# Decode attention plus MLP: wq loaded in eight DMAs, and two rows of wo in sixteen DMAs of falling size

## The chip, the cores and the metric

The kernel runs on one core of a Trainium2 chip. The core has a matrix engine (PE), three element-wise engines (DVE, ACT, POOL), a queue engine (SP) that only starts transfers, and sixteen DMA engines that move data between HBM and the on-chip memory SBUF, which has 128 partitions. The metric is device microseconds for one execution. Times before: 1281.98 and 1281.99 us in two runs, median 1281.99 us.

## What is computed

One decode step for 8 sequences (B = 8, one new token each, model width 640): a layer norm, then attention over a cache of 4096 keys with 32 heads of 128, plus a two-layer MLP on the same normalized input, plus the input itself.

```
xn = layernorm(x)                                   # x: 8 x 1 x 640
q  = xn @ wq                                        # wq: 640 x 4096
p  = softmax(q . k_cache / sqrt(128))               # k_cache, v_cache: 8 x 32 x 4096 x 128
A  = (p . v_cache) @ wo                             # wo: 4096 x 640
h  = gelu(layernorm(xn) @ w1 + b1)
out = x + A + h @ w2 + b2
```

All tensors are bf16. The two caches are 268 MB each, so nearly all of the bytes that the kernel moves are K and V, and each is read once.

## The kernel before

The work is cut into 32 groups (`NQ`): 8 heads of one sequence each. A group needs one K tile and one V tile, each 128 partitions x 65,536 bytes, 8 MB. SBUF has three slots of that size: K tiles alternate between two (`KA`, `KB`), V has the third (`VS`). All large transfers are started by SP, in one queue, in an order that is written out by hand: every step is registered with a position (`at(pos, step)`), the steps are sorted by it, and each engine gets its part of the list. A transfer may start when the slot is free: K tile i waits for the compute on K tile i-2 (`load_k`), V tile i for the product with V tile i-1 (`load_v`).

At the start the V slot holds the query weights wq: `load("wq", ...)` is the first transfer in SP's queue, 128 partitions of 40,960 bytes (5 rows of wq each). Behind it comes K tile 0. PE computes all queries from wq in one go (`pe_q`, 160 matmuls); K tile 1 and V tile 0 are issued only when that is done (`qmm`), since their slots hold the inputs. ACT's queue starts the small inputs: x (8 partitions), b2, and the last rows of w2 (`w2b`, 64 partitions).

At the end the output weights wo are loaded into a K slot, when the last K tile has been used. wo is cut by heads: `load_wl(0)` loads the first sixteen heads (2,560 KB), `load_wl(1)` the next eight (1,280 KB), and `load_wn` the last eight in three pieces. In these, a partition holds eight rows of wo (index s, 1,280 bytes each), and `WN_CUT = (0, 5, 7, 8)` cuts them: rows 0 to 4 (800 KB), rows 5 and 6 (320 KB: 128 partitions x 2,560 bytes), row 7 (160 KB). Each piece has its own semaphore, and PE adds it to the sum in `fin_wn(q)` when it has landed: 25, 10 and 5 matmuls. These 40 matmuls are the last real work; then the sum is cast (DVE), transposed (PE), copied (ACT) and stored.

So SP's queue reads: wq, K0, [wait for the queries] K1, V0, then K and V in turn, the MLP weights, V31, and behind the last wait five transfers of wo. A DMA adds 16 to its semaphore in all when it is complete, so that a wait for n DMAs on one semaphore is a wait for 16 n.

## Time and profile before

| | us |
|---|---|
| two timed runs | 1281.98, 1281.99 |
| profiled execution, first to last instruction | 1280.5 |
| DVE busy | 1103.8 |
| PE busy (matmul) | 671.1 |
| ACT busy | 476.6 |
| POOL busy | 106.3 |

The profiled execution is known by its span; the 1.5 us by which the timed runs are longer lie ahead of its first and behind its last instruction. DVE has the largest busy time of the compute engines, but 177 us less than the span. What is read off the profile below is mainly the state of the DMA engines: the share of time that the sixteen are busy, and the rate in GB/s, over the span and in chosen stretches. In a stretch, a packet is counted whole where it starts, so that short stretches give figures that swing, above 1 at places; they are used here over several packets, or where packets are short.

### The profile page before, as it was taken

The numbers are of one execution on the slowest core, as the hardware profiler recorded it, in microseconds if no ns is written. First come the engines' busy times: TensorE is split into PE (matmuls) and PEld (weight loads), VectorE is DVE, ScalarE is ACT, GpSimd is POOL, SyncE is SP. The second block draws the span as 40 slices with busy tenths as digits, with TensorE's granted clock in tenths as the row PEclk, the third lists the DMA queues.
The fourth block names the chain that finished last, engine by engine and source line by source line (L and its number), as shares of the span: only waits on it lengthen the run. The fifth ranks groups of instructions, "written<-read, shape, count | busy, mean of one in ns | idle before, by whom it ended". The sixth has DMA issues, their size and how long they took to land.

```text
span 1280.5 us, 34440 instructions
## 1 busy us (share of the span) xinstructions
PE 671.1 (52%) x13944; PEld 573.4 (45%) x13944; DVE 1103.8 (86%) x680; ACT 476.6 (37%) x904; POOL 106.3 (8%) x113
## 2 busy tenths in 40 slices
PE   1546555446545446545456554456454466464476
PEld 1435444335535345444345444345343355353365
DVE  1899999889888889888899888898888898888895
ACT  0524444233444233443234443234443234442331
POOL 0020010000000000000000000000000000000040
PEclk9755655566665565555565565566655555555655
DMA  9999999999999999999999999999999999999998
GB/s 419 431 426 435 426 436 432 442 426 436 432 440 428 434 432 438 432 432 430 436 438 426 434 434 442 426 434 434 438 430 430 430 440 436 428 432 436 433 437 361
DMA packets 10675, 551.99 MB, mean 431 GB/s; under 512 B 1244, under 2 KB 1445, under 8 KB 1702
## 3 DMA queue, kind: packets, MB, share of 16 engines
q1 hardware_dynamic: 10512, 551.70, 99.7%
q8 instruction: 9, 0.15, 0.0%
q10 hardware_dynamic: 150, 0.11, 0.0%
q14 instruction: 4, 0.03, 0.0%
HBM read 551.80 MB, written 0.01 MB: 431 GB/s over the span
## 4 chain that ended last, share of the span: by engine, by line
DMA 52%; DVE 36%; issue 11%; DVEq 0%; PE 0%; SPq 0%; ACT 0%
DMA S_sb<-in_A_k_cache_dram 51%; DVE S_sb L111 26%; DVE Sd_sb L111 8%; DMA S_sb<-in_A_wo_dram 2%; DVE S_ps L111 1%; DVE ri_sb L111 0%; DVEq L109 0%; PE ACC_ps L111 0%; DVE mx_sb L111 0%; SPq L111 0%; DVE mbT_sb L111 0%; DVE mxT_sb L111 0%; DVE mq_sb L111 0%; DVE mb_sb L111 0%; PE QB_ps L111 0%
## 5 line engine op out<-in xcount | busy, mean ns | idle before, releaser
L111 PE MATMUL TR_ps<-ident_bf,S_sb 128*128 128x128 bf16 (+1 forms) x2570 | 341.2, 273 | 354.1 <-POOL kr_sb L111 333.7
L111 DVE TENSOR_TENSOR S_sb<-S_sb,qbc_sb 128x7552 bf16<-128x7552 bf16 (+1 forms) x96 | 392.5, 4088 | 128.8 <-DMA S_sb<-in_A_k_cache_dram 128.4
L111 PEld LDWEIGHTS TR_ps<-ident_bf,S_sb 128*128 (+2 forms) x2570 | 243.6, 102 | 414.0 <-issue 338.2
L111 DVE TENSOR_REDUCE Sd_sb<-S_sb 128x59 f32<-128x3776 bf16 (+1 forms) x96 | 390.2, 4065 | 6.0
L111 ACT ACTIVATE KT_sb<-TR_ps 128x1024 bf16<-128x1024 bf16 x320 | 327.0, 1024 | 121.1 <-PE TR_ps L111 109.5
L111 PE MATMUL PV_ps<-P_sb,S_sb 128*128 128x8 bf16 x8192 | 224.0, 175 | 137.5 <-DMA S_sb<-in_A_v_cache_dram 134.5
L111 PEld LDWEIGHTS PV_ps<-P_sb,S_sb 128*128 128x128 bf16 x8192 | 221.4, 103 | 140.2 <-DMA S_sb<-in_A_v_cache_dram 137.0
L111 DVE TENSOR_TENSOR S_sb<-S_sb 128x3776 bf16<-128x3776 bf16 (+1 forms) x96 | 205.4, 2140 | 3.3
L111 ACT ACTIVATE P_sb<-Sd_sb,NB_sb 128x256 bf16<-128x256 f32 x256 | 126.3, 494 | 213.7 <-DVE NB_sb L111 213.7
L111 PE MATMUL S_ps<-qrep_sb,KT_sb 128*128 128x8 bf16 x2560 | 121.6, 177 | 51.6 <-ACT KT_sb L111 48.6
L111 ACT ACTIVATE oU_sb<-PV_ps 128x8 f32<-128x8 f32 x31 | 5.5, 178 | 376.8 <-PE PV_ps L111 376.8
L111 PEld LDWEIGHTS S_ps<-qrep_sb,KT_sb 128*128 128x128 bf16 x2560 | 91.3, 102 | 82.2 <-ACT KT_sb L111 41.6
L111 POOL TENSOR_TENSOR oT_sb<-oU_sb,ri_sb 128x8 bf16<-128x8 f32 x31 | 71.8, 2316 | 374.8 <-DVE S_sb L111 303.1
L111 POOL COPY qrep_sb<-qT_sb 128x128 bf16<-128x128 bf16 x32 | 19.2, 600 | 472.6 <-PE S_ps L111 454.0
L111 ACT ACTIVATION_READ_ACCUMULATOR P_sb<-Sd_sb,NB_sb 128x1 f32 x256 | 47.7, 186 | 0.0
L111 DVE TENSOR_TENSOR S_ps<-S_ps,mask_sb 128x320 f32<-128x320 f32 (+1 forms) x65 | 31.6, 486 | 2.6 <-PE S_ps L111 2.6
L111 DVE TENSOR_REDUCE Sd_sb<-S_ps 128x40 f32<-128x320 f32 x64 | 31.5, 492 | 2.2
L111 PE MATMUL QB_ps<-ident_bf,qrep_sb 128*128 128x128 bf16 x32 | 9.2, 286 | 40.7 <-DVE S_sb L111 21.2
L111 ACT ACTIVATE qbc_sb<-QB_ps 128x128 bf16<-128x128 f32 x32 | 8.9, 278 | 56.9 <-PE QB_ps L111 56.9
L111 POOL MEMSET kr_sb<- 128x1 f32 x32 | 3.2, 99 | 295.4 <-DMA S_sb<-in_A_k_cache_dram 295.4
L111 PEld LDWEIGHTS QB_ps<-ident_bf,qrep_sb 128*128 128x128 bf16 x32 | 3.3, 104 | 43.6 <-ACT oU_sb L111 29.3
L111 PE MATMUL CH_ps<-rs_sb,ones_f 128*128 128x8 f32 x64 | 16.7, 335 | 6.5 <-ACT P_sb L111 6.5
(73 smaller groups left out, 148.6 us busy)
## 6 DMA issues: line engine op xcount, KB each, us to landing
S_sb<-in_A_v_cache_dram SPq DMA_DIRECT2D x1, 6144.0 KB, 26.8
S_sb<-in_A_wq_dram SPq DMA_DIRECT2D x1, 5120.0 KB, 15.2
S_sb<-in_A_wo_dram SPq DMA_DIRECT2D x1, 2560.0 KB, 15.8
S_sb<-in_B_w_dram SPq DMA_DIRECT2D x1, 2160.0 KB, 30.3
S_sb<-in_B_w_dram SPq DMA_DIRECT2D x1, 2080.0 KB, 34.8
S_sb<-in_A_v_cache_dram SPq DMA_DIRECT2D x1, 2048.0 KB, 31.3
S_sb<-in_A_wo_dram SPq DMA_DIRECT2D x1, 1280.0 KB, 18.5
S_sb<-in_A_wo_dram SPq DMA_DIRECT2D x1, 800.0 KB, 20.0
```

The costliest lines, as they stand in the source:

```text
L111: inst = getattr(e, name)(*a, **k)
```

## The change

```
     WN_CUT = (0, 5, 7, HS)
+    ROWS_CUT = (15, 14, 13, 12, 11, 10, 9, 8, 8, 7, 6, 5, 4, 3, 2, 1)
...
+        def load_wq():
+            src = A_wq.rearrange("(p c) n -> p c n", c=DC)
+            for r in range(RW):
+                load("wq", ld_wq, wq_sb[r:P:RW], src[r:P:RW])
...
         def load_wn(q):
             lo, hi = WN_CUT[q], WN_CUT[q + 1]
             n = HS * DH
-            tk[("wn", q)] = ld_wn[q].sig(sp.dma_start(
-                woL_sb[:, 1, lo * D:hi * D],
-                A_wo[NL * n:(NL + 1) * n, :].rearrange("(p s) n -> p (s n)", p=P)[:, lo * D:hi * D]))
+            src = A_wo[NL * n:(NL + 1) * n, :].rearrange("(p s) n -> p (s n)", p=P)
+            a = 0
+            for k in ROWS_CUT if lo == WN_CUT[1] else (P,):
+                tk[("wn", q)] = ld_wn[q].sig(sp.dma_start(
+                    woL_sb[a:a + k, 1, lo * D:hi * D], src[a:a + k, lo * D:hi * D]))
+                a += k
...
-        at(-890, load, "wq", ld_wq, wq_sb, A_wq.rearrange("(p c) n -> p c n", c=DC))
+        at(-890, load_wq)
```

`RW` is 8. The one wq transfer of 128 partitions becomes eight transfers of 16 partitions: number r takes the partitions r, r + 8, r + 16 and so on to r + 120. All eight count on the semaphore of wq, and PE waits for the last of them, so for 128 in place of 16. Behind them K tile 0 follows in SP's queue as before.

The 320 KB piece of wo (rows 5 and 6 of the last eight heads) becomes sixteen transfers over consecutive partitions: 15 partitions, then 14, and so on down to 8, a second one of 8, and on to 1; 128 in all. They count on one semaphore, for which PE waits with 256 in place of 16. The 800 KB piece ahead and the 160 KB piece behind stay one DMA each.

Bytes, places in SBUF and all compute instructions are the same; SP's program has 22 more DMA instructions, the other engines' programs are unchanged.

## The prediction

> **What bounds the kernel now.** I read the page first, then SP's timeline, the DMA issues, the stretches, and the end of the chain of waits.

> ```profile
> span 1280.5 us, 34440 instructions
> ...
> DMA  9999999999999999999999999999999999999998
> ...
> q1 hardware_dynamic: 10512, 551.70, 99.7%
> ...
> HBM read 551.80 MB, written 0.01 MB: 431 GB/s over the span
> ```

> The digit line says that the sixteen DMA engines are busy in every slice; SP's queue (q1) alone keeps them busy for 99.7% of the span. The reader is to see that there is no slice with room in it: 551.7 MB at one constant rate are the time. DVE is in the chain of waits too, but what it waits for, and what waits for it, is the next tile. So an edit here is worth what it does to the first byte, to the rate, or to the last byte.

> The columns of the stretches below are the length, the busy time of PE, weight load, DVE, ACT and POOL, the granted clock, the DMA share and GB/s.

> ```profile
> 1.50:14.50 13.00, 1.22 (x21) 0.99 (x21) 5.00 (x22) 1.69 (x3) 0.78 (x8) 1.00 1.01 410
> 8.00:12.00 4.00, 0.56 (x13) 0.42 (x11) 0.18 (x1) 0.00 (x0) 0.00 (x0) 1.00 1.00 432
> 140.00:1240.00 1100.00, 585.85 (x12134) 499.02 (x12134) 970.07 (x566) 426.97 (x810) 86.39 (x86) 0.55 1.00 433
> ```

> From 8 to 12 us wq is under way, in rows of 40,960 bytes; from 140 to 1240 us K and V, in rows of 65,536. Both run at the same 432 to 433 GB/s, 27 GB/s for each of sixteen engines. A rate that doesn't care for the row length is that of a path of fixed width. Up to 14.5 us the mean is 410, so the first stretch of wq costs (1 - 410/432) x 13 = 0.7 us.

> ```profile
> 0.74 0.38 SPq L111 DMA_DIRECT2D S_sb<-in_A_wq_dram  x1
> 1.17 19.60 SPq L111 DMA_DIRECT2D S_sb<-in_A_k_cache_dram  x2
> 20.81 0.43 SPq L111 DMA_DIRECT2D S_sb<-in_A_v_cache_dram  x1
> ```
> ```profile
> 15.98 4.43 PE L111 MATMUL CH_ps<-xT_sb,S_sb 128*128 128x8 bf16 x160 [7.43 <-DMA S_sb<-in_A_wq_dram]
> ```
> ```profile
> S_sb<-in_A_wq_dram SPq DMA_DIRECT2D x1, 5120.0 KB, 15.2
> w2b_sb<-in_B_w_dram ACTq DMA_DIRECT2D x1, 80.0 KB, 13.9
> ...
> S_sb<-in_A_k_cache_dram SPq DMA_DIRECT2D x1, 34.8
> ```

> wq is issued at 0.74 us and lands 15.2 us later, and PE starts on it at 15.98. K0 stands behind it, issued at 1.17 and landed 34.8 us later: the engines go from wq to K0 without a pause. Whatever wq takes longer, everything behind it comes later by the same, since the queue is never empty again.

> **Part 1, wq in eight DMAs.** Removed: one issue of 0.38 us. Added: eight of that kind, 3.0 us, the last ending near 0.74 + 3.0 = 3.8 us. K0's issue moves from 1.17 to about 3.8, and that costs nothing: its bytes are wanted only when wq is through, near 15 us; 11 us of wq cover it. Each later piece has a cover too: a row of 40,960 bytes takes an engine 1.5 us at 27 GB/s, an issue 0.38. K1 and V0 wait for the queries as before, and K0's transfer covers that wait in both cases. The x, b2 and w2b loads go through ACT's queue and are not moved. In POOL's and PE's queues nothing moves, and the wait for 128 in place of 16 stands where the other stood.

> What can cost is the rate. The DMA is cut over the engines by partitions, as x shows, eight partitions, ahead of wq:

> ```profile
> DMA packets 6, 0.01 MB, mean 219 GB/s; under 512 B 0, under 2 KB 6, under 8 KB 6
> ...
> q10 hardware_dynamic: 6, 0.01, 124.8%
> ```

> That is the stretch from 1.700 to 1.735 us: six of its eight 1,280-byte rows start within 35 ns, so on different engines: one row, one engine. A 16-row piece gives each engine one row too. But these are rows 8 partitions apart, and which sixteen of SBUF's rows are written at the same time is new: before, an engine had eight rows of its own out of 128. If the path of fixed width is the engine's own, nothing is lost, and the first stretch may gain: between -0.7 us (its whole loss) and 0. If it is SBUF's side, shared by a set of partitions, then sixteen rows at a regular step need not lie on sixteen paths. With two on one path the rate is 216 GB/s: 5,120 KB (5.24 MB) take 24.3 us in place of 12.1, so +12.1. Bounds: -0.7 and +12.1 us. The rows of before hold no large load but those over 128 partitions, so they don't decide. I take two on one path, because a step of 8 in 128 is as regular as it can be, and each engine's eight pieces follow in the same order, so that two engines that meet go on meeting. From the 12.1 I take off the 0.7 of the slow first stretch, which half the rate hides: **+11.4 us**.

> [...]

> **Part 2, rows 5 and 6 of the last heads.**

> ```profile
> S_sb<-in_A_wo_dram SPq DMA_DIRECT2D x1, 2560.0 KB, 15.8
> S_sb<-in_A_wo_dram SPq DMA_DIRECT2D x1, 1280.0 KB, 18.5
> S_sb<-in_A_wo_dram SPq DMA_DIRECT2D x1, 800.0 KB, 20.0
> S_sb<-in_A_wo_dram SPq DMA_DIRECT2D x1, 320.0 KB, 20.3
> S_sb<-in_A_wo_dram SPq DMA_DIRECT2D x1, 160.0 KB, 20.2
> ```
> ```profile
> L111 SPq DMA_DIRECT2D S_sb<-in_A_wo_dram x5: 328/432/433, 1256.0 to 1257.8; - x5
> ```
> ```profile
> 1256.82 19.96 DMA S_sb<-in_A_wo_dram
> ...
> 1276.82 1.50 PE ACC_ps L111 x40
> ...
> 1278.35 0.21 DVE res_sb L111
> ```
> ```profile
> 1275.28 1.21 PE L111 MATMUL ACC_ps<-oS_sb,S_sb 128*128 128x8 bf16 x40
> 1276.82 1.49 PE L111 MATMUL ACC_ps<-oS_sb,S_sb 128*128 128x8 bf16 x40 [0.34 <-DMA S_sb<-in_A_wo_dram]
> ```

> Five issues of some 0.43 us each run from 1256.0 to 1257.8 (start of the last); sixteen in place of one add 15 x 0.43 = 6.5 us of SP, so the last starts near 1264.3. Its bytes are wanted at 1276 to 1277, when the others are through: about 12 us of V31 and wo cover it. Nothing else stands behind it on SP but the wait for the output. If that cover were gone it would cost up to 6.5 us.

> The chain ends with the 800 KB piece landing at 1276.78, then 40 matmuls. The same 40 took 1.21 us with everything there, and 1.49 here, so 0.28 us are waits for the later pieces: the last, issued at 1257.8, lands 20.2 us on, at 1278.0. A later landing there moves the end one for one; an earlier one gives 0.28 at most, as the 800 KB piece holds the start.

> ```profile
> 1275.50:1276.00 0.50, 0.50 (x25) 0.50 (x22) 0.43 (x2) 0.00 (x0) 0.00 (x0) 0.50 0.99 392
> 1276.00:1276.50 0.50, 0.49 (x19) 0.40 (x15) 0.00 (x0) 0.00 (x0) 0.00 (x0) 0.50 0.80 307
> 1276.50:1277.00 0.50, 0.18 (x6) 0.18 (x7) 0.00 (x0) 0.00 (x0) 0.00 (x0) 0.50 0.66 254
> 1277.00:1277.50 0.50, 0.50 (x25) 0.50 (x22) 0.00 (x0) 0.00 (x0) 0.00 (x0) 0.50 0.47 153
> ```

> The share falls from 0.99 to 0.47 over the last 1.5 us: the engines don't end together. The falling sizes move work: with one row to an engine, counted from the first, the first engine gets a row of all sixteen DMAs and the last none, where each had eight of 2,560 bytes (8 x 2,560 / 27 GB/s = 0.76 us). So the first engine ends 0.76 us later than now, the last 0.76 earlier. Whether the first ones are those that end early the rows don't say. Without meetings, this part gives between -0.28 and +0.76. With meetings, consecutive partitions may share a path: four rows on one, in lock-step, would make sixteen DMAs take 16 x 4 x 2,560 / 27 = 6.1 us, +5.3; the spread of 1.5 us in arrival breaks most of that up. I take half the rate, as for wq, for 320 KB: **+0.8 us**.

> **Sum.** The stretches are of an execution with a span of 1280.5 us; the timed runs are 1.5 us longer, around it, and nothing there changes. 1281.99 + 11.4 + 0.8 = 1294.2 us.

> **The rivals.**
> *No meeting* (not slower): the fixed path is each engine's own. For it: the constant rate fits that just as well. Against it: nothing but the regularity of the step. The time is 1281.99 with -0.7 to 0 for the first stretch and -0.28 to +0.76 for the end: 1281.0 to 1282.8, likeliest 1281.7. It decides as soon as a 16-row piece keeps 27 GB/s per engine.
> *Meeting at the end only*: neighbouring partitions share a path, partitions at a step of 8 or more don't. wq as now, the end +0.8 to +5.3, so 1282.8 to 1287.3, likeliest 1283.5. For it: the pieces of wo are consecutive partitions, those of wq far apart.
> *The pieces are not spread*: a 16-row DMA with this step runs on a quarter of the engines or paths. Then wq takes four times 12.1 us, +36.4, 1318 us. x's six rows in 35 ns speak against fewer engines. It passes 2% (25.6 us) from 0.32 of the rate on.

> **How the numbers follow.** Half rate at wq 0.62; no meeting 0.26; end only 0.07; not spread 0.03; the remaining 0.02 for what I don't see. The first case has a range of its own of 1291.5 to 1296.5 (two engines that meet drift apart and save up to 2; the end up to +3). Leaving out no-meeting would leave out too much, so the range goes from 1281.0 to 1296.5. A change of 2%, 25.6 us, is what is told from no change here; half rate and no meeting both stay under it, on either side of zero. More than 2% faster would need a stretch with idle DMA engines, and there is none: 0.01. More than 2% slower is the piece that isn't spread and unseen things: 0.04. Within: 0.95.

> **What would show it.** Right: the stretch from 8 to 12 us falls from 432 to about 216 GB/s, wq lands near 26.5 us and PE's 160 matmuls start there, K0's landing moves by the same 11 us, the stretch of K and V keeps 433 and its steps keep their length, and SP's sixteen issues end long before the last bytes. In the end the share falls over a longer time, with the 320 KB piece landing 0.8 us later against the 800 KB one. Wrong: 432 from 8 to 12 us and PE starting at 16 us or before; then the rest of the time is in the last 2 us, or a changed step in the middle would say that something other than wq's rate came in.

## The result: 15.5 us slower

The changed kernel takes 1297.51 us (1297.42 and 1297.60 in two runs) against 1281.99 us: +15.52 us, ratio 1.012, interval 1.0103 to 1.0136. The forecast was 1294.2 us with a range up to 1296.5; the direction and the mechanism held, the size did not.

The page of the changed kernel, and its stretches (columns as before: length, busy time of PE, weight load, DVE, ACT and POOL, granted clock, DMA share, GB/s):

```profile
span 1296.0 us, 34462 instructions
...
GB/s 229 440 427 428 435 431 437 431 435 435 431 437 431 435 433 433 435 433 433 435 433 431 435 433 437 433 429 437 433 435 431 433 437 433 431 435 433 429 438 341
...
q1 hardware_dynamic: 10736, 551.70, 99.6%
```
```profile
17.00:26.60 9.60, 0.00 (x0) 0.00 (x0) 0.00 (x0) 0.00 (x0) 0.00 (x0) 1.00 1.00 205
30.00:140.00 110.00, 53.58 (x1059) 45.19 (x1057) 88.70 (x48) 40.81 (x68) 6.76 (x9) 0.69 1.01 434
140.00:1240.00 1100.00, 579.24 (x11942) 492.12 (x11939) 970.27 (x576) 422.67 (x809) 88.54 (x88) 0.57 1.00 433
```

Of the forty slices only the first (229 GB/s, 419 before) has a much lower rate; the last is somewhat lower (341, 361 before). In wq's stretch all sixteen DMA engines are busy all the time, and move 205 GB/s. A busy share of 1.00 therefore says nothing of the rate here, as 432 GB/s had the same share before: in the trace's packet records a row of 40,960 bytes takes an engine 3.13 us in the mean here, and took 1.51 before, and all of it counts as busy. (From 8 to 12 us, the stretch that the forecast names, the view reads 261 GB/s at a share of 1.25, since packets are counted whole where they start; 261 / 1.25 = 209.) K and V run at 433 as they did.

SP's and PE's timelines of the changed kernel, at the start and at the end:

```profile
0.74 5.09 SPq L111 DMA_DIRECT2D S_sb<-in_A_wq_dram  x8
5.87 28.72 SPq L111 DMA_DIRECT2D S_sb<-in_A_k_cache_dram  x2
...
1270.07 7.46 SPq L111 DMA_DIRECT2D S_sb<-in_A_wo_dram  x20
```
```profile
29.80 4.43 PE L111 MATMUL CH_ps<-xT_sb,S_sb 128*128 128x8 bf16 x160 [21.39 <-DMA S_sb<-in_A_wq_dram]
...
1291.94 0.83 PE L111 MATMUL ACC_ps<-oS_sb,S_sb 128*128 128x8 bf16 x25 [1.31 <-DMA S_sb<-in_A_wo_dram]
1293.22 0.56 PE L111 MATMUL ACC_ps<-oS_sb,S_sb 128*128 128x8 bf16 x15 [0.45 <-DMA S_sb<-in_A_wo_dram]
```

PE starts the queries at 29.80 in place of 15.98 us: +13.8. SP's wait for the last K tile ends at 1270.07 in place of 1255.97: +14.1, so nothing was caught up or lost to speak of in 1240 us. The last 40 matmuls end at 1293.78 in place of 1278.31: +15.5. The time went to two places: 13.8 us into wq, some 1.4 us into the end, where the 40 matmuls, one run before, are now broken in two by waits.

### The profile page after: what moved, and what is told of

It is laid out like the page before. It is cut to its first block, busy times and chain, and to the rows that moved or that the text cites. A ratio compares the mean times of both kernels' runs of the same rounds, so it can differ in the third digit from the quotient of the medians.

```text
span 1296.0 us, 34462 instructions
## 1 busy us (share of the span) xinstructions
PE 670.8 (52%) x13944; PEld 572.6 (44%) x13944; DVE 1103.6 (85%) x680; ACT 476.4 (37%) x904; POOL 102.4 (8%) x113
## 2 busy tenths in 40 slices
DMA  9999999999999999999999999999999999999998
## 3 DMA queue, kind: packets, MB, share of 16 engines
q1 hardware_dynamic: 10736, 551.70, 99.6%
HBM read 551.80 MB, written 0.01 MB: 426 GB/s over the span
## 4 chain that ended last, share of the span: by engine, by line
DMA 52%; DVE 35%; issue 11%; SPq 1%; DVEq 0%; PE 0%; ACT 0%
DMA S_sb<-in_A_k_cache_dram 51%; DVE S_sb L111 26%; DVE Sd_sb L111 7%; DVE S_ps L111 1%; DMA S_sb<-in_A_wo_dram 1%; SPq L111 1%; DVE ri_sb L111 0%; DVEq L109 0%; DVE mx_sb L111 0%; DVE mbT_sb L111 0%; DVE mxT_sb L111 0%; DVE mq_sb L111 0%; PE ACC_ps L111 0%; DVE mb_sb L111 0%; PE QB_ps L111 0%
## 5 line engine op out<-in xcount | busy, mean ns | idle before, releaser
L111 PE MATMUL TR_ps<-ident_bf,S_sb 128*128 128x128 bf16 (+1 forms) x2570 | 340.4, 269 | 353.4 <-POOL kr_sb L111 337.8
L111 DVE TENSOR_TENSOR S_sb<-S_sb,qbc_sb 128x7552 bf16<-128x7552 bf16 (+1 forms) x96 | 392.4, 4088 | 129.1 <-DMA S_sb<-in_A_k_cache_dram 128.8
L111 PEld LDWEIGHTS TR_ps<-ident_bf,S_sb 128*128 (+2 forms) x2570 | 242.9, 102 | 414.1 <-issue 337.4
L111 DVE TENSOR_REDUCE Sd_sb<-S_sb 128x59 f32<-128x3776 bf16 (+1 forms) x96 | 390.2, 4065 | 6.0
L111 ACT ACTIVATE KT_sb<-TR_ps 128x1024 bf16<-128x1024 bf16 x320 | 326.9, 1024 | 121.2 <-PE TR_ps L111 109.8
L111 PE MATMUL PV_ps<-P_sb,S_sb 128*128 128x8 bf16 x8192 | 224.8, 175 | 138.8 <-DMA S_sb<-in_A_v_cache_dram 134.7
L111 PEld LDWEIGHTS PV_ps<-P_sb,S_sb 128*128 128x128 bf16 x8192 | 222.4, 103 | 141.5 <-DMA S_sb<-in_A_v_cache_dram 137.4
L111 DVE TENSOR_TENSOR S_sb<-S_sb 128x3776 bf16<-128x3776 bf16 (+1 forms) x96 | 205.4, 2140 | 3.3
L111 ACT ACTIVATE P_sb<-Sd_sb,NB_sb 128x256 bf16<-128x256 f32 x256 | 126.3, 494 | 213.5 <-DVE NB_sb L111 213.5
L111 PE MATMUL S_ps<-qrep_sb,KT_sb 128*128 128x8 bf16 x2560 | 121.9, 178 | 51.3 <-ACT KT_sb L111 48.2
L111 ACT ACTIVATE oU_sb<-PV_ps 128x8 f32<-128x8 f32 x31 | 5.5, 178 | 378.1 <-PE PV_ps L111 378.1
L111 PEld LDWEIGHTS S_ps<-qrep_sb,KT_sb 128*128 128x128 bf16 x2560 | 91.2, 102 | 81.6 <-ACT KT_sb L111 41.5
L111 POOL TENSOR_TENSOR oT_sb<-oU_sb,ri_sb 128x8 bf16<-128x8 f32 x31 | 71.6, 2310 | 379.0 <-ACT oU_sb L111 216.7
L111 POOL COPY qrep_sb<-qT_sb 128x128 bf16<-128x128 bf16 x32 | 15.5, 485 | 487.4 <-PE S_ps L111 454.9
L111 ACT ACTIVATION_READ_ACCUMULATOR P_sb<-Sd_sb,NB_sb 128x1 f32 x256 | 47.8, 187 | 0.0
L111 ACT ACTIVATE qbc_sb<-QB_ps 128x128 bf16<-128x128 f32 x32 | 8.9, 278 | 70.8 <-PE QB_ps L111 70.8
L111 DVE TENSOR_TENSOR S_ps<-S_ps,mask_sb 128x320 f32<-128x320 f32 (+1 forms) x65 | 31.5, 485 | 2.6 <-PE S_ps L111 2.6
L111 DVE TENSOR_REDUCE Sd_sb<-S_ps 128x40 f32<-128x320 f32 x64 | 31.5, 491 | 2.2
L111 PE MATMUL QB_ps<-ident_bf,qrep_sb 128*128 128x128 bf16 x32 | 9.2, 286 | 40.6 <-DVE S_sb L111 22.0
L111 POOL MEMSET kr_sb<- 128x1 f32 x32 | 3.2, 99 | 294.5 <-DMA S_sb<-in_A_k_cache_dram 294.5
L111 DVE CAST qT_sb<-CH_ps 128x256 bf16<-128x256 f32 x1 | 0.4, 424 | 26.1 <-PE CH_ps L111 26.1
L111 PEld LDWEIGHTS QB_ps<-ident_bf,qrep_sb 128*128 128x128 bf16 x32 | 3.3, 104 | 43.4 <-ACT oU_sb L111 28.8
## 6 DMA issues: line engine op xcount, KB each, us to landing
S_sb<-in_A_wo_dram SPq DMA_DIRECT2D x1, 2560.0 KB, 15.8
S_sb<-in_B_w_dram SPq DMA_DIRECT2D x1, 2080.0 KB, 34.8
S_sb<-in_A_wo_dram SPq DMA_DIRECT2D x1, 1280.0 KB, 18.5
```

What stands on the lines that cost most here:

```text
L111: inst = getattr(e, name)(*a, **k)
```

## The experiments

All times are compared with the kernel before as run on the same chip beside them (1282.01 us for the first four, 1281.86 for e5, e6 and e9, 1282.02 for e7 and e8, 1282.06 for the last three). Edits are shown against the kernel before.

**The two parts alone.** e1 has the changed kernel's `load_wq` and the old `load_wn`; e2 the reverse.

> Only wq is cut, into eight DMAs of 16 partitions at a step of 8; wo is loaded as before. If the two parts of the change add up, this has what the changed kernel lost by the start of its 160 query matmuls, 29.80 against 15.98 us, so +13.8: 1295.8 us, and the end as before. If the parts depend on each other (the engines' order at the end being set by the start), the sum of this run and the next differs from +15.5 by more than 0.5 us.

> Only rows 5 and 6 of the last heads are cut, into the sixteen DMAs of 15 to 1 partitions; wq is one DMA. From the changed kernel's end (its last landing to its last matmul, 1.4 us later against the start than before): 1283.4 us. A shared path for neighbouring partitions says +0.8 to +2; if the falling sizes only move work between engines, -0.3 to +0.8.

e1: 1296.21 us, +14.2, ratio 1.0108 (1.0079 to 1.0138). e2: 1284.02 us, +2.0, ratio 1.0015 (1.0004 to 1.0027). The sum, 16.2, is 0.7 above the 15.5 of both together. That passes the 0.5 us that the expectation set as the mark of parts that depend on each other, but e1's interval alone is some 3.8 us wide to either side, so whether they do stays open. wq is the large part.

**The number of DMAs, or the partitions?** e3 cuts wq by columns, e4 into two kinds of 16-row pieces.

```
+            dst, src = (t.rearrange("p c n -> p (c n)") for t in (wq_sb, src))     # e3
+            n = DC * H * DH // RW
+            for r in range(RW):
+                load("wq", ld_wq, dst[:, r * n:(r + 1) * n], src[:, r * n:(r + 1) * n])
...
+            for r in range(4):                                                     # e4
+                load("wq", ld_wq, wq_sb[32 + r:96:4], src[32 + r:96:4])
+            for lo in (0, 96):
+                for r in range(2):
+                    load("wq", ld_wq, wq_sb[lo + r:lo + 32:2], src[lo + r:lo + 32:2])
```

> wq is cut into eight DMAs again, but by columns: each takes all 128 partitions and 5,120 bytes of each. Shared path in SBUF: nothing lost, 432 GB/s from 8 to 12 us, 1281.3 to 1282.7 us. A price for each DMA of a cut transfer (some 1.7 us for each of eight): 1295.8 us.

> wq in eight DMAs of 16 partitions, in two kinds. The first four take partitions 32+r, 36+r and so on to 92+r (step 4 over partitions 32 to 95); the last four take every second partition of 0 to 31 or of 96 to 127. Shared path, with a path for four neighbours that is shared with the partitions 32 further on in the same half of 64: the first four pieces have sixteen paths and run at 432 GB/s, 1.5 us each, the last four have eight paths for sixteen rows, 3.2 us each: half of the loss of e1, +6.9, 1288.9 us. A price for each DMA of 16 rows: 1295.8 us, and the same rate from the first piece on.

e3: 1282.60 us, ratio 1.0004 (0.9992 to 1.0015), no difference to be told. Its stretch from 5 to 15 us, with eight DMAs, and its start of the queries:

```profile
5.00:15.00 10.00, 1.21 (x21) 0.99 (x21) 2.71 (x12) 0.20 (x1) 0.00 (x0) 1.00 1.02 419
```
```profile
16.44 4.43 PE L111 MATMUL CH_ps<-xT_sb,S_sb 128*128 128x8 bf16 x160 [7.51 <-DMA S_sb<-in_A_wq_dram]
```

That is 419 GB/s and not quite the expected 432, and the queries start 0.46 us later than before (15.98): a row of 5,120 bytes takes 0.196 us in the packet records, so eight of them 1.57, where one of 40,960 took 1.51.

e4: 1289.10 us, +7.1, ratio 1.0053 (1.003 to 1.0076), where half of e1's loss is 7.1. Its stretches:

```profile
4.50:9.00 4.50, 1.21 (x21) 0.99 (x21) 2.68 (x12) 0.20 (x1) 0.00 (x0) 1.00 0.95 401
9.50:21.50 12.00, 0.00 (x0) 0.00 (x0) 0.00 (x0) 0.00 (x0) 0.00 (x0) 1.00 0.94 210
```

Eight DMAs of 16 rows each, in one queue, of one size: the first kind runs at 401 GB/s, the second at 210. The large price here is not that of a DMA or of its 16 rows, but of the partitions that the 16 rows are in.

**Which partitions, and is it SBUF?** e5 takes 16 neighbours to a piece, e9 the step of e4's first kind from other places, e6 the changed kernel's partitions, read from other rows of HBM (so that its queries come out permuted).

```
+                load("wq", ld_wq, wq_sb[HW * r:HW * (r + 1)], src[HW * r:HW * (r + 1)])   # e5
...
+                load("wq", ld_wq, wq_sb[r:P:RW], src[HW * r:HW * (r + 1)])                # e6
...
+            for o in (0, 64):                                                             # e9
+                for r in range(4):
+                    load("wq", ld_wq, wq_sb[o + r:o + 64:4], src[o + r:o + 64:4])
```

> wq in eight DMAs of 16 neighbouring partitions (0 to 15, 16 to 31 and so on), the rows of wq adjacent in HBM as well. Shared path for four neighbours: sixteen rows on four paths, a quarter of the rate, 12.8 us for each pair of pieces less what engines apart in time save; 6.4 us a piece at most, so wq near 50 us, +36 to +40, 1318 to 1322 us. If the loss comes from rows far apart in HBM: none here, 1282 us. A price for each DMA of 16 rows: 1296 us.

> wq in eight DMAs of 16 partitions at a step of 8 in SBUF, as in the changed kernel, but read from 16 adjacent rows of HBM each (so the rows of wq are permuted, and the queries are others). Path in SBUF: 1296.2 us as e1. Rows apart in HBM as the cause: 1282 us.

> wq in eight DMAs of 16 partitions at a step of 4, four over the partitions 0 to 63 and four over 64 to 127: the same step as the first four pieces of e4, which start at partition 32. Path shared by partitions 32 apart in the same half of 64: eight paths for sixteen rows, 3.2 us a piece, 1296.2 us as e1. If the step decides, and not where it starts: the rate of e4's first pieces, 1282.5 us.

One run each, so without an interval: e5 1316.19 us (+34.3), e6 1294.91 us (+13.1), e9 1295.38 us (+13.5). The kernel before varied by less than 1 us in all its runs. The stretch in wq for e5, the same for e6, and for e9:

```profile
5.00:45.00 40.00, 1.26 (x21) 0.99 (x21) 2.98 (x13) 0.27 (x2) 0.00 (x0) 1.00 1.03 117
```
```profile
5.00:27.50 22.50, 1.06 (x21) 0.83 (x19) 2.22 (x9) 0.20 (x1) 0.00 (x0) 1.00 1.05 236
```
```profile
5.00:27.50 22.50, 1.06 (x21) 0.83 (x19) 2.22 (x9) 0.20 (x1) 0.00 (x0) 1.00 1.04 224
```

**The end.** e7 cuts the 320 KB piece into eight DMAs of sixteen neighbouring rows, with no work moved between engines; e8 moves work, in DMAs that were meant to have no two rows on one path.

```
+    ROWS_CUT = [slice(HW * r, HW * (r + 1)) for r in range(RW)]                              # e7
+    ROWS_CUT = [slice(o + r, o + n, 4) for o, n in ((32, 64), (0, 32), (96, 32)) for r in range(4)]   # e8
...
+            for s in ROWS_CUT if lo == WN_CUT[1] else (slice(0, P),):                        # both
+                tk[("wn", q)] = ld_wn[q].sig(sp.dma_start(
+                    woL_sb[s, 1, lo * D:hi * D], src[s, lo * D:hi * D]))
```

> wq as before; rows 5 and 6 of the last heads in eight DMAs of 16 neighbouring partitions: every engine still moves eight rows, so no work goes from one engine to another, but four rows meet on one path. Shared path: between the 320 KB at half rate (+0.8) and at a quarter (+2.3), and the last landing well behind the last packet, as in e2: 1282.8 to 1284.3 us. If what e2 loses comes from the falling sizes (first engine sixteen rows, last none): 1282.0 us.

> wq as before; the same 320 KB in twelve DMAs at a step of 4: four of 16 partitions over 32 to 95, four of 8 over 0 to 31, four of 8 over 96 to 127. No two rows of a DMA share a path, but the first eight engines get twelve rows and the last eight get four, where each had eight: the falling sizes' shift of work (0.4 us each way) without meetings. Shared path as the cause of e2's loss: 1281.7 to 1282.4 us. The shift, or the number of DMAs, as the cause: 1283 us or more.

e7: 1283.79 us (+1.8; 1.0015, 1.0004 to 1.0025). e8: 1284.01 us (+2.0; 1.0015, 1.0005 to 1.0024). Here the theory failed: e8, meant to be without meetings inside a DMA, loses as much as e2. What e2, e7 and e8 have in common is the number of completion signals of the cut piece, that is, of increments of its semaphore: 144, 128 and 136 in their traces, in place of 16. The last matmuls and the last stretches of e2, and the stretch of the kernel before in which its packets have ended:

```profile
1277.58 0.83 PE L111 MATMUL ACC_ps<-oS_sb,S_sb 128*128 128x8 bf16 x25 [1.02 <-DMA S_sb<-in_A_wo_dram]
1279.67 0.56 PE L111 MATMUL ACC_ps<-oS_sb,S_sb 128*128 128x8 bf16 x15 [1.26 <-DMA S_sb<-in_A_wo_dram]
```
```profile
1277.00:1278.00 1.00, 0.42 (x16) 0.43 (x17) 0.00 (x0) 0.00 (x0) 0.00 (x0) 0.50 0.60 170
1278.00:1278.50 0.50, 0.41 (x16) 0.32 (x12) 0.00 (x0) 0.00 (x0) 0.00 (x0) 0.50 0.04 13
1278.50:1279.00 0.50, 0.00 (x0) 0.00 (x0) 0.00 (x0) 0.00 (x0) 0.00 (x0) 0.50 0.00 0
1279.00:1279.50 0.50, 0.00 (x0) 0.00 (x0) 0.00 (x0) 0.00 (x0) 0.00 (x0) 0.50 0.00 0
```
```profile
1277.50:1278.00 0.50, 0.50 (x16) 0.41 (x13) 0.00 (x0) 0.00 (x0) 0.00 (x0) 0.50 0.00 0
```

From 1278.5 on no packet starts any more, and PE goes on waiting for a DMA until 1279.67. Before, packets started up to 1277.5, and PE had its last data at 1278.0. So the data are through, and the landing is reported more than a microsecond later. The traces show it signal by signal: each is a packet of 4 bytes, and the last one of all landed 0.4 us after the last such packet before, and 1.5 us after it in e2. Hence the last three: the piece cut by columns, in four and in eight DMAs, where no rows meet and no work moves; and the same number of signals in a piece that ends some 6 us earlier.

```
+            m = 4 if lo == WN_CUT[1] else 1                                        # e10; e11: 8
+            w = (hi - lo) * D // m
+            for a in range(lo * D, hi * D, w):
+                tk[("wn", q)] = ld_wn[q].sig(sp.dma_start(woL_sb[:, 1, a:a + w], src[:, a:a + w]))
...
+            m = 8 if q == 0 else 1                                                 # e12, in load_wl
+            w = (hi - lo) * D // m
+            for a in range(0, (hi - lo) * D, w):
+                tk[("wl", q)] = ld_wl[q].sig(sp.dma_start(dst[:, a:a + w], src[:, a:a + w]))
```

> wq as before; the 320 KB of rows 5 and 6 in four DMAs by columns (128 partitions, 640 bytes of each): no rows meet on a path, no work moves between engines, 64 completion signals of engines in place of 16. Signals that land one after the other as the cause of the +1.8 to +2.0 of e2, e7 and e8 (128 signals each): some 48/112 of it, +0.8, 1282.8 us, with the last landing 0.8 us or so behind the last packet (before: 0.4). Meetings or moved work as the cause: 1282.0 us.

> The same in eight DMAs by columns (128 partitions, 320 bytes of each): 128 signals, as in e2, e7 and e8, but no meetings and no moved work. Signals as the cause: +1.8 to +2.2, 1283.8 to 1284.2 us. Meetings or moved work as the cause: 1282.0 us, with up to 0.3 for the shorter rows.

> rows 5 and 6 in one DMA as before; it is the 2,560 KB piece of wo, which ends some 6 us before the last one, that is cut into eight DMAs by columns: 112 more signals, in the six microseconds of its own transfer, with the later pieces behind them. Signals that bunch up at the end as the cause: they have landed long before, 1282.0 to 1282.3 us. A fixed price for each DMA wherever it stands: +1.8, 1283.8 us.

e10: 1282.42 us (+0.4; 1.0002, 0.9993 to 1.0012: not to be told from no change). e11: 1283.27 us (+1.2; 1.001, 1.0000 to 1.0019). e12: 1282.59 us (+0.5; 1.0005, 0.9995 to 1.0014: not to be told from no change, and above what was expected). PE and the stretches at the end of e11, and PE at the end of e12:

```profile
1276.94 0.83 PE L111 MATMUL ACC_ps<-oS_sb,S_sb 128*128 128x8 bf16 x25 [0.45 <-DMA S_sb<-in_A_wo_dram]
1278.67 0.56 PE L111 MATMUL ACC_ps<-oS_sb,S_sb 128*128 128x8 bf16 x15 [0.91 <-DMA S_sb<-in_A_wo_dram]
```
```profile
1277.50:1278.00 0.50, 0.27 (x10) 0.18 (x7) 0.00 (x0) 0.00 (x0) 0.00 (x0) 0.50 0.36 110
1278.00:1278.50 0.50, 0.00 (x0) 0.00 (x0) 0.00 (x0) 0.00 (x0) 0.00 (x0) 0.50 0.00 0
1278.50:1279.00 0.50, 0.33 (x12) 0.33 (x13) 0.00 (x0) 0.00 (x0) 0.00 (x0) 0.50 0.00 0
```
```profile
1277.57 1.49 PE L111 MATMUL ACC_ps<-oS_sb,S_sb 128*128 128x8 bf16 x40 [0.72 <-DMA S_sb<-in_A_wo_dram]
```

In e11 the 25 matmuls on the 800 KB piece start at 1276.94, nearly as before (1276.82); the last 15 wait until 1278.67, 0.7 us after the last packet's stretch. Eight DMAs instead of one at the end cost 1.2 us with neither meetings nor moved work, less than the 1.8 to 2.2 expected, and with an interval that just reaches zero. Not all of it is signals. In e11's trace, whose run is 0.9 us longer, the last row ends 0.3 us later than before, as rows of 320 bytes are slow: 0.020 us each, so eight take 0.16, and one of 2,560 took 0.10. The signals add some 0.6: the last lands 1.0 us after its packet, in place of 0.4. (SP's last four issues took 1.7 to 5.2 us each in e11, but the last ended at 1273.7, and the engines stayed full until the data ran out.)

In e10 and e12 the signals are not late: the last lands 0.4 and 0.5 us after its packet. What these two may have lost is in the rows, whose last one ends 0.2 us later than before in e10 (rows of 640 bytes) and 0.7 in e12 (1,024 rows of 2,560 bytes at 0.10 us, in place of 128 of 20,480 at 0.76). So late signals are seen where the cut piece has 128 or more in the last 3 to 4 us, and not with 64 there, nor with 128 spread over some 7 us of an earlier piece. Short rows did not make them late here: e2, e7 and e8 have none, and e10, with rows of 640 bytes, has its last signal 0.4 us after its packet.

Of e2's 2.0 us e11 leaves some 0.8, and the timelines show where: in e2 the 25 matmuls start at 1277.58, 0.64 us later than in e11, and so they do in e7 (1277.58) and e8 (1277.45). In all three the piece in front, which was not touched, lands late. (In e12 the matmuls start as late, but there every piece of wo is late by the same 0.7 us.)

e7's and e8's rows for these 25 matmuls:

```profile
1277.58 0.83 PE L111 MATMUL ACC_ps<-oS_sb,S_sb 128*128 128x8 bf16 x25 [0.99 <-DMA S_sb<-in_A_wo_dram]
```
```profile
1277.45 0.83 PE L111 MATMUL ACC_ps<-oS_sb,S_sb 128*128 128x8 bf16 x25 [0.81 <-DMA S_sb<-in_A_wo_dram]
```

That fits rows that meet across DMAs: the engines arrive 1.5 us apart, and one that is ahead, already in the cut piece, writes into partitions whose path an engine behind may still need for the 800 KB piece. The packet records bear it out: the longest of this piece's rows of 6,400 bytes took 0.38, 0.42 and 0.40 us in e2, e7 and e8, and 0.25 before and in e10, e11 and e12, the three with cuts by columns. So e8 was not free of meetings either. By these records the piece's last row ended 0.5, 0.7 and 0.3 us later than before in e2, e7 and e8; the rest of its delay, up to 0.3 us, is the signal's. No run takes this meeting alone.

## Why the prediction missed

- *The kernel is bound by the rate of its DMA engines, and a delay at the start stays.* Right: +13.8 at the queries, +14.1 at the last K tile, K and V at 433 GB/s.
- *The added issues of SP cost nothing.* Right but for the first one (0.4 us, below), though wq's took longer than worked out: the eight took 5.1 us and not 3.0, and K0's issue came at 5.87 and not near 3.8; wq's transfer, which ran to 29 us, covered them. At the end twenty issues took 7.5 us, some 12 us ahead of their need.
- *Two rows on one path halve wq's rate: +12.1, less 0.7 for the slow first stretch, +11.4.* The mechanism held, and the rivals fell: no meeting by the 205 GB/s, meeting at the end only by e1, a quarter of the engines by the share of 1.00 and by e4. **The mis-sized term is this one: 13.8 us in place of 11.4.** That two rows of a piece would meet was the author's choice, which no row of before shows; the changed kernel showed 205 GB/s. The sum took the transfer at exactly half the rate and nothing else. The packet records of the two traces show where the missing 2.4 us are:

| part of the delay at wq | before | changed | more than forecast |
|---|---|---|---|
| the first row starts at | 1.76 us | 2.13 us | 0.37 us |
| an engine's eight rows take, in the mean | 12.79 us | 25.08 us | 0.86 us (+12.29, forecast +11.43) |
| pauses between rows, and the engines ending apart | 1.03 us | 1.88 us | 0.85 us |
| from the last row's end to PE's start | 0.40 us | 0.71 us | 0.31 us |

The second line is the rate below half: a row took 3.13 us in the mean, and not twice 1.51. To the first line belongs that the issues are not "of that kind": each of wq's took at least 0.57 us, in place of 0.38; in e5, whose first took 0.38, the first row starts at 1.78. What makes the third and the fourth longer stays open. The range's upper end fell with the term, as it stood on half the rate as a bound. The sign "near 26.5 us" for PE's start didn't fit the sum even so: 15.98 + 11.4 is 27.4.
- *Half the rate hides the slow first stretch.* Right. Before, the first row of each engine took 2.19 us in the mean and the later ones 1.51, which is the 0.7; in the changed kernel the first took 3.14 and the later ones 3.13. So from 1.5 to 5.0 us the rate fell below that of the rest only before (below: before, then changed).

```profile
1.50:5.00 3.50, 0.01 (x1) 0.01 (x1) 2.67 (x13) 1.49 (x2) 0.78 (x8) 1.00 1.08 377
```
```profile
1.50:5.00 3.50, 0.15 (x4) 0.16 (x5) 2.69 (x14) 1.49 (x2) 0.78 (x8) 1.00 1.03 214
```

- *The end: +0.8, from rows that meet.* 1.4 us in the changed kernel, 2.0 alone. Here a cause was missing: the last signal of all landed 1.5 us after its packet in e2, whose cut piece has 144 of them, and 1.0 us after it in e11, with 128, in place of 0.4 before, with 16. The wait for 256 in place of 16 was taken as one wait like the other; e11 loses 1.2 us with no meetings to be seen; its trace, of a run that is 0.9 longer, gives 0.3 to shorter rows and 0.6 to the signals. Whether the falling sizes set the engines' ends right, as their order would be for, can't be read off: e7, without them, loses about the same. The gain that could be had was bounded at 0.28 us by the 40 matmuls.
- *Within 2%.* Right: 1.2%.

No variant beat the kernel before; e3, e10 and e12 are as fast within their intervals.

## What to carry to other kernels

Before cutting a DMA by partitions, write down which partitions its engines write at the same time. Here pieces of sixteen rows ran at 401 GB/s at a step of 4 over partitions 32 to 95 (e4), at 224 at the same step within one half of the 128 (e9), at 205 at a step of 8 over all of them, at 210 at a step of 2 within 32 (e4) and at 117 as neighbours (e5). Cutting by columns kept 419 GB/s (e3) and cost little away from the end: e3 and e12 lost 0.6 and 0.5 us, within their intervals. At the very end of a kernel count completion signals as well as bytes: with 144 of them for the cut piece the last of all landed 1.5 us after its packet (e2), with 128 1.0 us after (e11), with 16 0.4 us after (before).

## What was not expected of the hardware

A row of 40,960 bytes takes 1.51 us in the kernel before, 3.13 us in the changed kernel and 5.72 us in e5. If these are one, two and four rows at a time on a path, as the author reads the rates, the path moves 27, 26 and 29 GB/s: two engines on it get a little less together than one alone, and four a little more. The DMA share reads 1.00 to 1.03 all the while (before, from 8 to 12 us: 1.00; changed: 1.00; e5: 1.03). And completion signals took time that no data packet shows: with 112 to 128 more of them in the last 3 to 4 us, PE waited over a microsecond (e2) or 0.8 us (e11) after the last packet. In the changed kernel's trace the last 64 of the cut piece's 144 signals landed a median of 0.0125 us apart, as if they stood in line. With 48 more (e10) they were not late: the last landed 0.4 us after its packet.
